# Clustered attention and its MoE layer: later chunks' query scale clipped, centroids' norm by Newton steps, a new order of work

## The chip, the cores and the metric

One core of one Trainium2 chip runs the whole program. The metric is the device time of one execution in microseconds (us). The kernel before took 847.42 us, the median of 3 runs (845.54 to 848.62). Five engines matter here: TensorE (PE, with its weight loads as PEld), VectorE (DVE), ScalarE (ACT), GpSimd (POOL), and SyncE (SP), whose one queue issues all DMAs of the loops.

## The reference

Four batches, eight heads, 768 tokens, head dimension 64, 16 centroids per head. Queries and keys are each given to the centroid with the largest cosine, and a query sees only keys of its own cluster. The outputs of all heads go through a two-layer network with the weights w_in (512 x 2048) and w_out (2048 x 512), which arrive as 64-bit floats.

```python
c_n = centroids / (np.linalg.norm(centroids, axis=-1, keepdims=True) + 1e-06)
q_assign = np.argmax(np.einsum('bhsd,hcd->bhsc', q_n, c_n), axis=-1)
k_assign = np.argmax(np.einsum('bhsd,hcd->bhsc', k_n, c_n), axis=-1)
mask = q_assign[:, :, :, None] == k_assign[:, :, None, :]
scores = np.where(mask, (1.0 / np.sqrt(D)) * np.matmul(q, k.transpose(0, 1, 3, 2)), -1e9)
attn = np.exp(scores - max);  attn = attn / (sum + 1e-09)
out = np.matmul(attn, v)
h = x @ w_in                      # x: the heads side by side, (3072, 512)
g = np.where(h >= 1, h, np.where(h <= -1, 0.0, (h + 1) ** 2 / 4))
return g @ w_out
```

## The kernel before

**Tiling.** Heads are taken in four pairs. The queries of a batch are cut into three chunks (c = 0, 1, 2) of 256 tokens, so there are 12 chunks, numbered u = 3b + c. For a chunk and a head pair there are four steps of scores (two heads, two blocks of 128 queries): four matmuls of 384 columns give the scores of 128 queries against 768 keys in PSUM, VectorE evicts them with a running minimum (tile sS), ScalarE takes the exponential, the result is split into a high and a low half-precision part (ScalarE, GpSimd), transposed by DMA, and multiplied with V. A finished chunk goes through the network in eight parts (ffn1, ffn2 of 256 hidden units each).

**Two stages.** Before its first use every weight has to be brought from 64-bit to 32-bit floats. `w_bits` does it with ScalarE (magnitudes) and VectorE (bit merges of 1024 words a partition), and only chunk 0 uses those 32-bit weights directly. Chunk 0's attention, the weights and the preparation of batch 0's keys and values share the opening; afterwards weights are split into two half-precision parts and all else runs from those.

**Scales.** Numbers are split into half-precision parts after a scaling by a power of two. `k_scale` (L807) keeps for each head pair the inverse scale `ik` and the scale `sc`; `q_scale` (L881) does so for the queries of a chunk (`iv`, `sc`). `q_split` (L896) forms the high and low parts of the scaled queries in the tile qn, and their transposes give `qT`. In `q_pairs` (L913) the one-hot of the cluster is appended, with the weight `ONE`, so that keys of other clusters fall out. The score's scale `es` is the product of the two inverse scales and the reference's 1/8, held away from zero at `ES_MIN`; where it is held, the factor phi = raw / es makes up for it, and it is multiplied into the queries everywhere: on GpSimd into the high part in its natural layout (4 instructions a chunk, the product taking the low part's place in the tile), on ScalarE into the transposed queries in place (4 a chunk). In chunks with c = 0 `q_pairs` is called once for each head pair, in the others once for all four.

**Centroids.** `centroids()` (L690) is the first work recorded: the sum of squares on VectorE, a square root on ScalarE, then the reciprocal and the scaling on VectorE, a split, and a DMA transpose into `cT`, which the first label matmuls read. The activation on the tile `tab` (L685 and L697) uses a function early so that its table is loaded before it is needed: Sqrt at the start, Exp after the norm.

**The order.** Nothing is issued as it is written. A recorder collects instructions as nodes of a graph with planned costs (`price`). `issue` (L391) runs a planner: `BASE` rounds of a forward pass (`forward`, the engine takes the ready node of the best priority) and a backward pass (`backward`, which gives every node a priority by its distance from the end). Then a list of seeds, `NUDGES`, moves the priorities of groups of events (an event is one call such as one head pair's `k_split`); `nudge` (L377) turns a seed into a group, a stride and a shift. A last forward pass fixes the order of every engine and of the DMA queue. Each instruction then waits for its data by semaphores. As all instructions go through the recorder, the profile puts them all on L405, and tiles tell them apart.

Of the kernel before, what the change touches and what calls it, by code (L numbers as in the profile page):

```python
# [11 lines left out]
F32 = mybir.dt.float32  # L12
# [34 lines left out]
BASE = 20  # L47
NUDGES = (
# [59 lines left out]


def mix(a):  # L110

    a &= 0xFFFFFFFF
    a ^= a >> 16
    a = a * 0x7FEB352D & 0xFFFFFFFF
    a ^= a >> 15
    a = a * 0x846CA68B & 0xFFFFFFFF
    return a ^ a >> 16


class Recorder:  # L120
# [256 lines left out]
    def nudge(self, seed, prio):  # L377

        a = mix(seed * 2654435761 + 1)
        b = mix(a + 1)  # L380
        c = mix(b + 1)
        names = sorted({x.ev for x in self.nodes})
        lo, every, size = b % len(names), (1, 2, 5)[(a >> 8) % 3], float(500 << ((a >> 16) % 5))
        at = {y: i for i, y in enumerate(names)}
        for x in self.nodes:
            i = at[x.ev]
            if lo <= i < lo + (1 << (a % 8)) and not (i - lo) % every:
                r = c if c >> 8 & 1 else mix(c + i * 7919)
                prio[x] += ((r & 0xFFFF) / 32768.0 - 1.0) * size

    def issue(self):  # L391
        for x in self.nodes:
            for y in x.preds:
# [172 lines left out]
def tile_clustered_attention_moe(  # L566
# [17 lines left out]
    P = 128  # L584
# [881 lines left out]
```

## Time and profile before

| | |
|---|---|
| device time, median of 3 runs | 847.42 us (845.54 to 848.62) |
| span of the profiled execution, first to last instruction | 844.9 us |
| the profiled execution's own time | not listed |
| TensorE matmuls busy | 807.8 us (96%), 7100 instructions |
| VectorE busy | 628.9 us (74%), 1390 instructions |
| ScalarE busy | 667.1 us (79%), 1175 instructions |
| GpSimd busy | 528.7 us (63%), 510 instructions |
| mean granted TensorE clock | 0.994 of full speed |
| bytes moved by DMA | 142.50 MB |

Busy time is the time in which an engine executes; the rest of the span it waits or has nothing to do. The profile's chain of waits, followed back from the last instruction, is 85% TensorE and 6% VectorE. The span in 40 slices shows TensorE at nine tenths or more from the fifth slice on and at two to seven tenths in the first four. Below, "idle before <-" is the time that an engine stood still in front of an instruction, and the instruction that ended it.

### The profile page before, as it was taken

How to read it: one execution, taken by the hardware profiler on the slowest of the kernel's cores; microseconds unless marked ns; L12 is line 12 of the kernel's file. 1: busy time of each engine (PE TensorE's matmuls, PEld its weight loads, DVE VectorE, ACT ScalarE, POOL GpSimd, SP SyncE). 2: the span in 40 equal slices, each digit the busy share in tenths (PEclk: the TensorE clock that was granted, in tenths of full speed). 3: DMA queues.
4: the chain of work that ended last, by engine and by line, in shares of the span. 5: the costliest groups of instructions: out<-in, count | busy, mean ns of one | idle time of the engine just before them, and what ended most of it. 6: DMA issues, size and time to landing. Idle time of an engine off the chain costs nothing.

```text
span 844.9 us, 18910 instructions
## 1 busy us (share of the span) xinstructions
PE 807.8 (96%) x7100; PEld 563.2 (67%) x7100; DVE 628.9 (74%) x1390; ACT 667.1 (79%) x1175; POOL 528.7 (63%) x510
## 2 busy tenths in 40 slices
PE   2677999999999999999999999999999999999998
PEld 2455677667676767666666767666676676667776
DVE  5999998788888758669888758678888767454331
ACT  7889999999988778788778778788778778776332
POOL 1012589888878668666667667666757668666312
PEclk9999999999999999999999999999999999999999
DMA  9977898979999799889999979999988767666100
GB/s 313 295 187 179 241 225 192 182 156 198 207 170 183 149 160 175 173 181 207 203 159 179 157 149 175 188 189 193 212 161 145 154 135 141 129 128 103 24 26 26
DMA packets 404907, 142.50 MB, mean 169 GB/s; under 512 B 372816, under 2 KB 396624, under 8 KB 404816
## 3 DMA queue, kind: packets, MB, share of 16 engines
q1 hardware_dynamic: 404816, 141.30, 82.0%
q8 instruction: 55, 0.90, 0.4%
q14 instruction: 36, 0.29, 0.1%
HBM read 40.40 MB, written 6.29 MB: 55 GB/s over the span
## 4 chain that ended last, share of the span: by engine, by line
PE 85%; DVE 6%; issue 2%; DMA 1%; ACT 1%; POOL 1%; SPq 0%; DVEq 0%; POOLq 0%; ACTq 0%
PE pair L405 42%; PE banka L405 12%; PE bankj L405 11%; PE banki L405 11%; PE bankh L405 9%; DVE sS L405 1%; DMA kv<-n 1%; DVE w L405 1%; DVE bankj L405 1%; DMA pT<-hl 1%; POOL hl L405 0%; DVE wk L405 0%; DVE x L405 0%; DVE mx L405 0%; DVE bankh L405 0%
## 5 line engine op out<-in xcount | busy, mean ns | idle before, releaser
L405 POOL TENSOR_TENSOR hl<-sS,hl 128x768 f16<-128x768 f32 x176 | 299.0, 1702 | 118.3 <-ACT hl L405 99.0
L405 PE MATMUL pair<-w,g 128*128 128x512 f16 (+2 forms) x1120 | 275.9, 387 | 0.0
L405 DVE CUSTOM_DVE_ANT_0 sS<-pair,zero,er 128x768 f32<-128x768 f32 x192 | 194.4, 1013 | 71.5 <-PE pair L405 57.7
L405 PEld LDWEIGHTS <-w 128*128 128x128 f16 x2112 | 205.6, 98 | 41.2 <-issue 2.0
L405 ACT ACTIVATE sS<-sS,sbi 128x768 f32<-128x768 f32 x192 | 179.1, 933 | 67.5 <-DVE sbi L405 64.9
L405 PEld LDWEIGHTS <-g 128*128 128x128 f16 x1104 | 105.5, 98 | 101.8 <-issue 1.4
L405 PE MATMUL pair<-kv,q 128*128 128x384 f16 x768 | 159.7, 332 | 5.6 <-ACT pT L405 3.3
L405 ACT CAST hl<-sS 128x768 f16<-128x768 f32 x176 | 144.7, 826 | 7.8 <-DMA pT<-hl 5.6
L405 POOL TENSOR_TENSOR g<-r,g 128x512 f16<-128x512 f32 x80 | 95.8, 1198 | 54.7 <-ACT g L405 54.5
L405 PEld LDWEIGHTS <-q 128*128 128x128 f16 x992 | 78.7, 98 | 62.8 <-issue 20.4
L405 PE MATMUL banka<-pT,kv 128*64 128x256 f16 (+1 forms) x1680 | 104.8, 279 | 0.0
L405 PEld LDWEIGHTS <-kv 128*64 128x64 f16 (+1 forms) x1824 | 92.6, 108 | 6.5 <-DMA kv<-n 2.6
L405 ACT ACTIVATE r<-r,f_ra,f_rs 128x512 f32<-128x512 f32 x80 | 64.8, 810 | 25.4 <-DVE r L405 24.8
L405 PE MATMUL bankj<-x,w 128*128 128x256 f16 (+1 forms) x424 | 58.3, 289 | 0.9 <-DVE r L405 0.9
L405 ACT CAST g<-r 128x512 f16<-128x512 f32 x80 | 48.9, 611 | 8.1 <-DVE r L405 7.1
L405 POOL TENSOR_TENSOR qn<-qn,phi 128x256 f16<-128x256 f16 x48 | 31.7, 676 | 36.3 <-DVE phi L405 27.2
L405 PE MATMUL bankh<-x,w 128*128 128x256 f16 (+1 forms) x376 | 46.7, 277 | 0.0
L405 PE MATMUL banki<-x,w 128*128 128x256 f16 (+1 forms) x288 | 40.0, 290 | 0.0
L405 ACT ACTIVATE q<-q,phi 128x512 f16<-128x512 f16 x48 | 33.6, 717 | 5.0 <-DVE phi L405 4.9
L405 PE MATMUL banki<-wk,w 128*128 128x256 f16 x312 | 37.2, 273 | 0.0
L405 ACT ACTIVATION_READ_ACCUMULATOR sS<-sS,sbi 128x1 f32 x192 | 36.1, 188 | 0.0
L405 POOL CAST rr<-rs 128x4 f16<-128x4 f32 x48 | 13.2, 276 | 36.1 <-DVE bankh L405 13.7
(269 smaller groups left out, 1114.8 us busy)
## 6 DMA issues: line engine op xcount, KB each, us to landing
w<-in_moe_w_out_dram SPq DMA_DIRECT2D x14, 512.0 KB, 5.8
q<-in_q_dram SPq DMA_DIRECT2D x12, 512.0 KB, 4.8
kv<-in_k_dram SPq DMA_DIRECT2D x16, 384.0 KB, 4.3
kv<-in_v_dram SPq DMA_DIRECT2D x16, 384.0 KB, 4.6
out_dram<-o SPq DMA_DIRECT2D x11, 512.0 KB, 3.6
w<-in_moe_w_in_dram SPq DMA_DIRECT2D x10, 512.0 KB, 7.3
word<-in_moe_w_in_dram SPq DMA_DIRECT2D x6, 512.0 KB, 6.0
o<-in_v_dram SPq DMA_DIRECT2D x8, 384.0 KB, 4.0
```

What stands on the lines that cost most here:

```text
L405: fn(*args, **kw)
```

## The change

Three things change. In chunks with c = 1 and 2 the queries' inverse scale `iv` is held from below, in `q_scale`, by a number worked out from the keys' scale `sk`, so that the score's scale is never under `ES_MIN`; the score's scale `es` is worked out there too, and phi, its GpSimd and its ScalarE multiplications are left out. The tile's low part is replaced by a copy of the high part on VectorE. Chunks with c = 0 stay as they were. `k_scale` keeps its scales in a tile for all four pairs (`sk`), in place of one small tile each.

The norm of the centroids is worked out on VectorE: a starting guess of 1/sqrt from the bits of the sum of squares, three Newton rounds of three instructions, and one product. The only early activation is an Exp.

The order comes from 37 rounds in place of 20, and from a list with one shift for every event, `SHIFTS`, added once to the priorities, in place of the seeds.

```diff
-BASE = 20
-NUDGES = (
-    4127111602, 1682835989, 681108749, 3292080817, 121738153, 2216588642, 619074244, 589741012, 2371205860,
...
+BASE = 37
+SHIFTS = (
+    -1711, 7131, 3865, 6139, 639, -10363, 2153, 2349, 9056, -1055, 6506, -1469, -561, 1610, 4832, -13174, -6658, 2275,
...
     def issue(self):
...
-        for seed in NUDGES:
-            self.nudge(seed, prio)
+        names = sorted({x.ev for x in self.nodes})
+        shift = dict(zip(names, SHIFTS, strict=True))
+        for x in self.nodes:
+            prio[x] += shift[x.ev]
         self.forward(prio)
...
-    rec.scalar.activation(out=tab, in_=ones[:, :1], func=AF.Sqrt)
+    rec.scalar.activation(out=tab, in_=ones[:, :1], func=AF.Exp, scale=0.0)
 
     def centroids():
...
-        nrm = const.tile([P, 1], F32, name="c_nrm")
-        rec.scalar.activation(out=nrm, in_=ss, func=AF.Sqrt)
-
-        rec.scalar.activation(out=tab, in_=nrm, func=AF.Exp, scale=0.0)
-        rn = const.tile([P, 1], F32, name="c_rn")
-        rec.vector.tensor_scalar(out=rn, in0=nrm, scalar1=1e-6, scalar2=None, op0=ALU.add)
+        rn, y, m = (const.tile([P, 1], F32, name=f"c_{x}") for x in ("rn", "y", "m"))
+
+
+        rec.vector.tensor_scalar(
+            out=y.bitcast(U32), in0=ss.bitcast(U32), scalar1=-0.5, scalar2=float(0x5F3759DF), op0=ALU.mult, op1=ALU.add
+        )
+        for _ in range(3):
+            rec.vector.scalar_tensor_tensor(out=m, in0=y, scalar=ss, in1=y, op0=ALU.mult, op1=ALU.mult)
+            rec.vector.tensor_scalar(out=m, in0=m, scalar1=-0.5, scalar2=1.5, op0=ALU.mult, op1=ALU.add)
+            rec.vector.tensor_tensor(out=y, in0=y, in1=m, op=ALU.mult)
+        rec.vector.tensor_scalar(out=rn, in0=ss, scalar1=y, scalar2=1e-6, op0=ALU.mult, op1=ALU.add)
         rec.vector.reciprocal(rn, rn)
...
-        sc = e["sc"] = new("sc", [1], F32, 2)
+        sc = e["sc"] = BX[b]["sk"][:, hp : hp + 1]
...
         rec.vector.tensor_scalar(out=iv, in0=ar, scalar1=TINY, scalar2=2.0**-11, op0=ALU.max, op1=ALU.mult)
+        if u % NCH:
+            f = BX[u // NCH]
+            es = e["es"] = new("es", [NP], F32, 2)
+            rec.vector.scalar_tensor_tensor(
+                out=iv, in0=f["sk"], scalar=ES_MIN / QK, in1=iv, op0=ALU.mult, op1=ALU.max
+            )
+            rec.vector.scalar_tensor_tensor(
+                out=es, in0=f["ik"], scalar=-QK, in1=iv, op0=ALU.mult, op1=ALU.mult
+            )
         rec.vector.reciprocal(sc, iv)
...
+        if c:
+            es = e["es"][:, pairs]
+            rec.vector.tensor_copy(nat[:, x, 0], nat[:, x, 1])
+        else:
+            raw, es = (ps[:, i * NP : i * NP + m] for i in range(2))
+            ph = new("phi", [NP], F32, 2)[:, :m]
...
```

## Rows read from the trace of the kernel before

**Rows 1.** Busy time by stretch: engines' busy us, granted clock, DMA share, GB/s.

```profile
0.00:15.00 15.00, 4.39 (x54) 3.67 (x55) 5.62 (x19) 9.44 (x17) 2.55 (x27) 1.00 0.88 283
15.00:95.00 80.00, 58.91 (x586) 40.32 (x582) 77.05 (x188) 70.31 (x111) 14.33 (x21) 0.94 0.90 244
95.00:800.00 705.00, 703.01 (x6153) 488.37 (x6152) 534.17 (x1168) 574.34 (x1030) 502.58 (x455) 1.00 0.86 167
800.00:845.00 45.00, 41.53 (x317) 30.82 (x315) 12.07 (x16) 12.99 (x20) 9.20 (x8) 1.00 0.06 24
```

**Rows 2.** Timeline, VectorE's long wait: start, us, instruction, [idle before <-releaser].

```profile
15.23 0.95 DVE L405 TENSOR_REDUCE v_am<-kv 128x1 bf16<-128x768 f32 x1 [2.78 <-DMA kv<-in_v_dram]
```

**Rows 3.** Timeline of TensorE, 78 to 102 us.

```profile
84.41 0.87 PE L405 MATMUL pair<-idf,sS 128*128 128x128 f32 x6 [1.43 <-ACT sS L405]
...
95.48 3.62 PE L405 MATMUL banki<-x,w 128*128 128x256 f32 x16
```

**Rows 4.** Timeline of VectorE, 78 to 102 us.

```profile
90.89 1.16 DVE L405 TENSOR_REDUCE aq<-q 128x4 bf16<-128x1024 f32 x1
91.98 0.94 DVE L405 TENSOR_REDUCE v_am<-x 128x1 bf16<-128x768 f32 x1
92.84 1.00 DVE L405 CUSTOM_DVE_ANT_0 sS<-pair,zero,er 128x768 f32<-128x768 f32 x1
```

**Rows 5.** VectorE's groups, 15 to 95 us: shape, count, busy us, mean ns.

```profile
L405 DVE SCALAR_TENSOR_TENSOR w<-w,o 128x1024 uint32<-128x1024 uint32 x5 | 6.1, 1222 | 0.0
...
L405 DVE SCALAR_TENSOR_TENSOR w<-word,wk 128x1024 uint32<-128x1024 uint32 x1 | 1.2, 1208 | 0.0
```

**Rows 6.** Timeline, all engines, the centroids' chain and the first labels.

```profile
6.25 0.08 DVE L405 DVE_READ_ACCUMULATOR2_ANT c_ss<- 128x1 f32 x1
...
7.63 0.19 ACT L405 ACTIVATE c_nrm<-c_ss 128x1 f32<-128x1 f32 x1
...
7.85 0.15 DVE L405 TENSOR_SCALAR c_rn<-c_nrm 128x1 f32<-128x1 f32 x1 [1.04 <-ACT c_nrm L405]
...
9.11 1.28 SPq L405 DMA_TRANSPOSE cT<-sS  x1
...
9.96 1.89 PE L405 MATMUL pair<-idf,qn 128*128 128x128 bf16 x16 [2.02 <-DVE qn L405]
...
10.48 0.92 ACT L405 ACTIVATE n<-kv,sc 128x768 f16<-128x768 f32 x1
11.42 1.28 ACT L405 ACT_TABLE_LOAD   x1
...
12.82 1.91 ACT L405 COPY q<-pair 128x1024 bf16<-128x1024 bf16 x2
...
13.87 0.60 PE L405 MATMUL bankj<-cT,q 128*128 128x16 f16 x16
...
14.79 0.60 PE L405 MATMUL bankj<-cT,q 128*128 128x16 f16 x16 [0.32 <-ACT q L405]
```

**Rows 7.** Timeline of VectorE, two dependent one-column instructions.

```profile
29.15 0.17 DVE L405 RECIPROCAL phi<-banki 128x1 f32<-128x1 f32 x1
29.35 0.16 DVE L405 TENSOR_TENSOR phi<-banki,phi 128x1 f32<-128x1 f32 x1
```

**Rows 8.** View of the tile cT: issue to landing.

```profile
DMA to landing us min/median/max: 4.5/4.5/4.5
```

**Rows 9.** View of the tile phi: ns min/median/max, first and last start.

```profile
L405 POOL TENSOR_TENSOR qn<-qn,phi x48: 603/612/1591, 20.3 to 701.0; 128x256 f16<-128x256 f16 x48
L405 ACT ACTIVATE q<-q,phi x48: 705/717/754, 20.8 to 708.9; 128x512 f16<-128x512 f16 x48
```

**Rows 10.** Timeline of VectorE, the one-hot of chunk 1's queries.

```profile
79.67 0.28 DVE L405 TENSOR_SCALAR qn<-zs 128x256 f16<-128x256 f32 x1
```

**Rows 11.** VectorE's groups by shape, whole span: the same conversion.

```profile
L405 DVE TENSOR_SCALAR qn<-zs 128x256 f16<-128x256 f32 x8 | 5.0, 626 | 0.1
```

**Rows 12.** Timeline of ScalarE, 78 to 90 us.

```profile
83.32 0.94 ACT L405 ACTIVATE sS<-sS,sbi 128x768 f32<-128x768 f32 x1 [0.24 <-DVE sbi L405]
```

More of the change, by code (lines that the diff above doesn't have):

```diff
@@ L46 @@
 LOOK, MARGIN = 0.4, 4000
-BASE = 20
-NUDGES = (
[56 rows of a table removed]
+BASE = 37
+SHIFTS = (
[54 rows of a table added]
 )
 TILED = 248
[L110 to L117, printed above, removed]
 class Recorder:
@@ L375, in backward @@
         return start
[L377 to L389, printed above, removed]
     def issue(self):
@@ L811, in k_scale @@
         if hp == 0:
-            BX.setdefault(b, {}).update(ik=new("ik", [NP], F32, 2), has=new("has", [NP, 2, C], F32))
+            BX.setdefault(b, {}).update(
+                ik=new("ik", [NP], F32, 2), sk=new("sk", [NP], F32, 2), has=new("has", [NP, 2, C], F32)
+            )
         am = new("am", [1], F32, 2)
@@ L893, in q_scale @@
         rec.vector.tensor_scalar(out=iv, in0=ar, scalar1=TINY, scalar2=2.0**-11, op0=ALU.max, op1=ALU.mult)
+        if u % NCH:
[6 more added lines that the diff above has]
+                out=es, in0=f["ik"], scalar=-QK, in1=iv, op0=ALU.mult, op1=ALU.mult
+            )
         rec.vector.reciprocal(sc, iv)
@@ L921, in q_pairs @@
         ps = misc(512)
-        raw, es, ri = (ps[:, i * NP : i * NP + m] for i in range(3))
         zq = view(ps[:, 64 : 64 + m * SC * C], [2 * m, CT, C], F32)
-        ph = new("phi", [NP], F32, 2)[:, :m]
-        rec.vector.scalar_tensor_tensor(
-            out=raw, in0=f["ik"][:, pairs], scalar=-QK, in1=e["iv"][:, pairs], op0=ALU.mult, op1=ALU.mult
-        )
-        rec.vector.tensor_scalar(out=es, in0=raw, scalar1=-ES_MIN, scalar2=None, op0=ALU.min)
-        rec.vector.reciprocal(ph, es)
-        rec.vector.tensor_tensor(out=ph, in0=raw, in1=ph, op=ALU.mult)
-        for i in range(m):
-            y = slice((hp + i) * SC, (hp + i + 1) * SC)
-            rec.gpsimd.tensor_tensor(
-                out=nat[:, y, 0], in0=nat[:, y, 1], in1=ph[:, i : i + 1].unsqueeze(2).to_broadcast([P, SC, D]), op=ALU.mult
-            )
-            qf = e["qT"][:, y].rearrange("p n q -> p (n q)")
-            rec.scalar.activation(out=qf, in_=qf, func=AF.Copy, scale=ph[:, i : i + 1])
+        if c:
[4 more added lines that the diff above has]
+            ph = new("phi", [NP], F32, 2)[:, :m]
+            rec.vector.scalar_tensor_tensor(
+                out=raw, in0=f["ik"][:, pairs], scalar=-QK, in1=e["iv"][:, pairs], op0=ALU.mult, op1=ALU.mult
+            )
+            rec.vector.tensor_scalar(out=es, in0=raw, scalar1=-ES_MIN, scalar2=None, op0=ALU.min)
+            rec.vector.reciprocal(ph, es)
+            rec.vector.tensor_tensor(out=ph, in0=raw, in1=ph, op=ALU.mult)
+            for i in range(m):
+                y = slice((hp + i) * SC, (hp + i + 1) * SC)
+                rec.gpsimd.tensor_tensor(
+                    out=nat[:, y, 0], in0=nat[:, y, 1], in1=ph[:, i : i + 1].unsqueeze(2).to_broadcast([P, SC, D]),
+                    op=ALU.mult,
+                )
+                qf = e["qT"][:, y].rearrange("p n q -> p (n q)")
+                rec.scalar.activation(out=qf, in_=qf, func=AF.Copy, scale=ph[:, i : i + 1])
         rec.vector.tensor_scalar(
```

108 rows, old and new, of tables (NUDGES, SHIFTS) are left out of this document.

## The prediction, made before the result was known

> **What bounds the kernel now.** I read the busy time by stretch first, because shares over the whole span mix stages with different limits. The sums of [rows 1] are to be read as TensorE idle time: 15.00 - 4.39 = 10.6 us before 15 us, 80.00 - 58.91 = 21.1 us from 15 to 95 us, 705.00 - 703.01 = 2.0 us from 95 to 800 us, and 45.00 - 41.53 = 3.5 us at the end; together 37.2 us, and 807.8 us of matmuls. From 95 us on TensorE is the bound: it is busy 99.7% of 705 us at the full clock of 2.4 GHz (granted 1.00), while ScalarE is busy 81%, VectorE 76% and GpSimd 71%. Work taken from those three there is worth nothing until it removes some of the 2.0 us. The last 3.5 us is one eviction and the store behind the last matmul.
>
> The stretch from 15 to 95 us is another kernel, and VectorE bounds it: 77.05 of 80 us busy, 2.95 us idle in all. Its one long wait, 2.78 us for the first V load, ends at 15.23 us and so lies almost wholly ahead of the stretch [rows 2]. ScalarE is close behind with 70.31 us; GpSimd has only 14.33. The granted clock is 0.94 there, so some 0.06 x 2 x 80 = 10 us ran at 1.2 GHz, which matters little while VectorE is late. What ends the stretch is told by the timeline: the first hidden-layer product of chunk 0 starts at 95.48 us with a 16-matmul group and from there TensorE never rests [rows 3]; it needs the four attention outputs of chunk 0, and in front of the last two score evictions (92.84 us) VectorE does a reduction of 1.16 us for chunk 2's queries and one of 0.94 us for the next batch's V [rows 4]. Neither is needed before 95 us. Twenty bit merges of weights, 1.22 us each, 24.5 us in all, are in the stretch too (the first and the last group of them in [rows 5]); that is where the order decides.
>
> **The change, part by part.** The matmuls stay as they are, 7100 of them, so TensorE's 807.8 us is a floor that nothing moves. The sum is made against the profiled execution: its span is 844.9 us, its own time is not listed, and the median of three runs is 847.4, so I add 2.5 us to any span.
>
> *Centroids.* Removed from ScalarE: the square root and the Exp on one element, 0.19 us each by the former's row, and the table load between two kinds of function, 1.28 us, together 1.66 us [rows 6]. It stands in a busy place: the K split ends at 11.40, the load runs from 11.42, and the copy of the transposed queries starts only at 12.82, though TensorE had transposed the queries by 9.96 + 1.89 = 11.85. Added to VectorE: one starting guess and three rounds of three, ten dependent instructions. Two dependent instructions on one column start 0.20 us apart [rows 7], so the norm is there 10 x 0.20 = 2.0 us after the sum of squares (6.33 us): 8.33 us against 7.85 now, 0.5 us later, and up to 0.8 us if the two instructions of the query scale stand between. The transposed centroids are issued at 9.11 and land 4.5 us after [rows 8], at 13.6 us, and the first label matmul starts at 13.87. So this wait, hidden behind ScalarE's copies by 0.2 us today, is what comes late next: landing at 14.1 to 14.4 us. All 32 label matmuls then run in one go, 1.2 us, and end at 15.3 to 15.6 us where they ended at 15.39. For the labels the two halves cancel: nothing. What is left is ScalarE's 1.66 us before 20 us, in a stage where it is the busier engine and prepares the magnitudes that VectorE merges later. The bounds are 1.66 us gained and 0.8 us lost; I take 0.7 us gained, under half, since VectorE, which ScalarE feeds, has only 2.95 us of idle time to give back before 95 us, and its wait before that is for a load.
>
> A rule of the Trainium skill gives this another price. The rows show a load of 1.28 us and the next activation running straight behind it [rows 6]. "ScalarE: Activation LUTs", What ACT_TABLE_LOAD costs, charges a switch of set with a drain of about 1.38 us as well, 2.66 us in total. By that rule ScalarE would be 1.38 us freer still and, at the same share, the gain 1.3 in place of 0.7 us, the time 843.8; here the trace disagrees, as no such gap stands around the load.
>
> *The factor phi.* It goes for 8 of 12 chunks: 32 of 48 GpSimd multiplications at a median 0.61 us and 32 of 48 ScalarE scalings at 0.72 us [rows 9], 20 and 23 us. With them go four small VectorE instructions a chunk (in the one call for all pairs); two new ones stand in the scale's step and one copy of 1024 half-precision numbers in place of the multiplication. The copy's price is not in the trace. From below: a conversion of 256 numbers into the same tile took 0.28 us with GpSimd idle [rows 10]; from above: the same conversion has a mean of 0.63 over the run [rows 11], where GpSimd competes, and 1.22 us is a two-input pass over 1024 words [rows 5]. I take 0.45 us, near the lower end, as in the opening GpSimd is idle. VectorE so pays -2 x 0.16 + 0.45 = +0.1 us a chunk, between -0.1 and +0.9. The copy has to wait until the queries' transpose has read the tile, as GpSimd's multiplication did; behind that nothing urgent stood on GpSimd, while on VectorE the next score eviction (1.00 us in [rows 4]) is queued, and TensorE waits for its bank. The upper bound is taken for that too.
> Seven of the eight chunks are prepared after 95 us, where TensorE is the bound: they give nothing. Chunk 1 alone is prepared in the opening. There ScalarE loses 4 x 0.72 = 2.9 us between 80 and 85 us, and TensorE does wait 1.43 us for a score exponential at 84.41 [rows 3]; but that exponential was itself waiting 0.24 us for VectorE [rows 12], so most of the wait is VectorE's. I take 0.4 us gained less 0.1 us for the copy: 0.3 us, with bounds of 0.9 us lost and 1.4 us (that wait) gained. Transposed queries no longer scaled in place can be read sooner, which takes part of the 2.0 us between 95 and 800 us: 0.3 us of it.
>
> *The order.* A priority list worked out anew moves everything, the loads and transposes on SP's one queue included, with less ScalarE and GpSimd work to place. No row prices it; the stretch bounds it. The two early reductions put behind 95 us are worth 1.16 + 0.94 = 2.1 us. Each weight merge put behind the last score eviction of chunk 0 is worth 1.22 us more, and each put ahead costs as much. I take 1.7 us gained: most of the two reductions, none of the merges. Its bounds are four merges more either way: 2.1 + 4.9 = 7.0 us gained, 4.9 us lost.
>
> Sum: 0.7 + 0.3 + 0.3 + 1.7 = 3.0 us; span 841.9 us, time 847.4 - 3.0 = **844.4 us**.
>
> **Rivals.** *The relief is hidden.* VectorE, not the relieved engines, bounds the opening, and TensorE the rest; the work on VectorE is the same to 2 us. Then only the 0.3 us from 95 us on remains: 847.1 us. For it speaks that 95 of 100 us of freed work lies where nobody waits; against it, that the centroid step frees ScalarE at its fullest.
> *The order brings chunk 0's products much earlier.* Both reductions and four merges go behind 95 us: 847.4 - 7.0 = 840.4 us. For it: 21.1 us of TensorE idle time lies in 80 us, and GpSimd, idle there, cannot be the limit. Against: the second-layer weights have to be merged in time for their own products, and the loads keep the DMA engines 0.90 busy.
> *The order puts VectorE work ahead of chunk 0's last scores.* The place is VectorE's queue before 95 us; each merge more costs 1.22 us there, and the other terms give 1.3 us back. From three on (3.7 - 1.3 = +2.4 us) it decides; with four 847.4 + 4.9 - 1.3 = 851.0 us. For it: an order fitted to planned costs can meet other ones on the chip, and VectorE has no slack to absorb it. Against: any list that does so leaves TensorE idle in its own plan.
>
> **How the numbers follow.** Forecast 0.42, with its own range from 842.5 to 846.5; hidden 0.21; much earlier 0.22; slower 0.15. The range should leave out half of the slower case and a third of the much earlier one: 839.0 to 849.5 us; it takes in the bounds of the copy and of the Newton chain. A measurement of this kernel tells 0.3% from no change, that is 2.5 us: faster is below 844.9, slower above 850.0. Faster: some 0.6 of the forecast's 0.42, all of 0.22 and a little of the hidden case, 0.51. Slower: 0.11, most of its case. Same: the rest, 0.38.
>
> **What would show it.** One table load in place of two, ten one-column instructions between the centroids' sum and their norm, and the transposed centroids landing after 14 us. TensorE's idle time from 95 us to the end within 0.5 us of today's 5.5; the whole difference in the opening. VectorE's busy time from 15 us to the first product of chunk 0 shorter by about 2 us, and that product at about 92.5 to 93 us, with the reductions for chunk 2 and the next batch behind it. GpSimd near 509 us and ScalarE near 642 us busy. I am wrong if the first product starts later than 95 us, if TensorE opens gaps of over 2 us after it, or if the busy time of TensorE itself changes.

## The result, and the profile after

The changed kernel took 853.31 us (median of 4 runs, 852.58 to 853.76), the kernel before on the same chip 847.61 us (4 runs, 845.54 to 848.62): ratio 1.0077, 95% interval 1.0062 to 1.0091. It is slower by some 6 us; the prediction of 844.4 us, its range up to 849.5 and its sign were wrong. The profiled execution of after has a span of 850.8 us and a time of 852.58 us, so 1.8 us lie around the span; the prediction had added 2.5.

Busy time of after by stretch, to be laid beside [rows 1] (stretch, its length, busy us of PE, PEld, DVE, ACT, POOL with counts, granted clock, DMA share, GB/s):

```profile
0.00:15.00 15.00, 3.96 (x32) 3.05 (x33) 8.01 (x31) 9.29 (x15) 2.48 (x27) 1.00 0.85 297
15.00:95.00 80.00, 59.08 (x589) 40.54 (x588) 73.98 (x181) 65.02 (x104) 8.94 (x17) 0.96 0.84 227
95.00:800.00 705.00, 699.93 (x6120) 484.46 (x6120) 532.68 (x1166) 558.21 (x1000) 484.37 (x426) 1.00 0.87 168
800.00:851.00 51.00, 47.38 (x362) 35.21 (x360) 13.64 (x19) 14.97 (x22) 10.34 (x9) 0.98 0.06 21
```

TensorE's idle time up to 95 us is 32.0 us, where it was 31.7. From 95 us on it is 5.07 + 3.42 = 8.5 us up to the end of the span, which lies 0.2 us before the end of the last row; it was 2.0 + 3.4 = 5.4. Its busy time rose by 2.5 us to 810.35 with the same 7100 matmuls; that alone is no sign of a loss, as in clip_no_copy_old_order below, which is no slower than the kernel before, they take 810.1 us. So 3.4 us more idle and 2.5 us more busy make the 5.9 us of the span. The opening was not idle for longer, but less was done in it: 14 matmuls that stood before 95 us come after it, six of scores and eight on a weight tile (TensorE's groups, 0 to 95 us, before and after: count | busy us, mean ns | idle just before, its releasers):

```profile
L405 PE MATMUL pair<-kv,q 128*128 128x384 f16 x86 | 20.9, 375 | 4.8 <-ACT pT L405 3.3 <-ACT kv L405 0.6 <-DVE sbi L405 0.6
L405 PE MATMUL bankj<-wk,ones 128*128 128x128 bf16 x16 | 1.2, 218 | 0.0
```

```profile
L381 PE MATMUL pair<-kv,q 128*128 128x384 f16 x80 | 19.8, 387 | 7.5 <-ACT pT L381 4.3 <-DMA kv<-x 2.0 <-ACT kv L381 1.1
L381 PE MATMUL bankj<-wk,ones 128*128 128x128 bf16 x8 | 0.6, 218 | 0.0
```

By these rows 1.1 + 0.6 = 1.7 us of work were pushed behind 95 us, so some 2 of the 5.9 us come out of the opening and some 4 arise after it. The first hidden-layer product does not show that share: it starts at 95.75 us against 95.48 [rows 3], and from there to the end of the span, the pushed-back work included, it is 850.8 - 95.75 = 755.1 us against 749.4. The relief came nearly as counted (ScalarE busy 647.5 us, GpSimd 506.1, where 642 and 509 were named), and nothing was faster for it.

What VectorE does in front of chunk 0's last scores, beside [rows 4], and the first product (timelines of VectorE and TensorE, after):

```profile
91.11 1.01 DVE L381 CUSTOM_DVE_ANT_0 sS<-pair,zero,er 128x768 f32<-128x768 f32 x1
92.05 1.21 DVE L381 TENSOR_REDUCE aq<-q 128x4 bf16<-128x1024 f32 x1
93.18 0.94 DVE L381 TENSOR_REDUCE v_am<-x 128x1 bf16<-128x768 f32 x1
94.04 1.01 DVE L381 CUSTOM_DVE_ANT_0 sS<-pair,zero,er 128x768 f32<-128x768 f32 x1
...
95.75 3.62 PE L381 MATMUL banki<-x,w 128*128 128x256 f32 x16
```

The two reductions that the prediction sent behind 95 us stand where they stood.

The centroids' chain, beside [rows 6] (timeline of VectorE, SyncE and TensorE, after):

```profile
5.48 0.15 DVE L381 TENSOR_SCALAR c_y<-c_ss 128x1 uint32<-128x1 uint32 x1
5.67 0.22 DVE L381 SCALAR_TENSOR_TENSOR c_m<-c_y,c_ss 128x1 f32<-128x1 f32 x1
6.93 0.14 DVE L381 TENSOR_SCALAR c_m<-c_m 128x1 f32<-128x1 f32 x1
...
9.90 0.21 DVE L381 TENSOR_SCALAR c_rn<-c_ss,c_y 128x1 f32<-128x1 f32 x1
...
12.01 1.28 SPq L381 DMA_TRANSPOSE cT<-sS  x1
15.96 1.00 PE L381 MATMUL bankj<-cT,q 128*128 128x16 f16 x32
```

The ten instructions begin 0.2 us apart where they follow each other, but the new order puts other work between them (1.26 us from the second to the third). The transpose goes out at 12.01 in place of 9.11 us, and the first label matmul waits until 15.96 in place of 13.87.

The clip's new instructions (VectorE's groups by shape, whole span: count | busy us, mean ns | idle just before, its releaser):

```profile
L381 DVE SCALAR_TENSOR_TENSOR iq<-sk,iq 128x4 f32<-128x4 f32 x8 | 5.6, 700 | 0.2
L381 DVE COPY qn<-qn 128x1024 f16<-128x1024 f16 x8 | 4.0, 499 | 7.2 <-DMA q<-qn 7.2
L381 DVE SCALAR_TENSOR_TENSOR es<-ik,iq 128x4 f32<-128x4 f32 x8 | 3.9, 487 | 0.0
```

The copy takes 0.50 us, near the 0.45 that was priced, but VectorE stands still for 7.2 us in front of the eight copies, for the queries' transpose. The two small instructions, priced at 0.16 us, take 0.49 and 0.70 on average.

TensorE's longest wait after the opening lies at 213 us (timeline of after, all engines; in brackets the wait in front of the instruction and what ended it):

```profile
205.74 2.12 POOL L381 TENSOR_TENSOR w<-word,w 128x1024 f16<-128x1024 f32 x1
205.83 2.12 DVE L381 TENSOR_TENSOR bankh<-zs,has 128x64 f32<-128x64 f32 x1
207.86 0.15 DVE L381 RECIPROCAL sk<-ik 128x1 f32<-128x1 f32 x1
208.05 0.94 ACT L381 ACTIVATE n<-kv,sk 128x768 f16<-128x768 f32 x1 [1.98 <-DVE sk L381]
...
210.21 1.42 SPq L381 DMA_TRANSPOSE kv<-n  x1
...
215.61 0.47 PE L381 MATMUL bankh<-cT,kv 128*128 128x32 f16 x12 [2.04 <-DMA kv<-n]
```

An addition on 64 columns, 0.22 us at its shortest in this kernel, lasts as long as GpSimd's pass beside it; the key scale queued behind it is 2 us late, and ScalarE, the transpose and TensorE pass that on. The Trainium skill, "SBUF — State Buffer", Who interferes with whom, says that a VectorE instruction with two SBUF inputs contends with a GpSimd instruction that reads SBUF, and that such contention is an exclusive lock. The two rows of 2.12 us agree: both inputs of the addition lie in SBUF, and it ends 0.1 us behind GpSimd's pass.

### The profile page after: what moved, and what is told of

It is laid out like the page before. It is cut to its first block, busy times and chain, and to the rows that moved or that the text cites. A ratio compares the mean times of both kernels' runs of the same rounds, so it can differ in the third digit from the quotient of the medians.

```text
span 850.8 us, 18823 instructions
## 1 busy us (share of the span) xinstructions
PE 810.4 (95%) x7100; PEld 563.3 (66%) x7100; DVE 628.3 (74%) x1392; ACT 647.5 (76%) x1140; POOL 506.1 (59%) x478
## 4 chain that ended last, share of the span: by engine, by line
PE 74%; DVE 9%; DMA 8%; ACT 4%; issue 3%; POOL 1%; SPq 0%; DVEq 0%; ACTq 0%; POOLq 0%
PE pair L381 37%; PE banka L381 11%; PE bankj L381 9%; PE bankh L381 9%; PE banki L381 8%; DMA pT<-hl 2%; DVE sS L381 2%; DMA kv<-x 1%; DMA kv<-n 1%; ACT sS L381 1%; DVE r L381 1%; DVE bankj L381 1%; DVE qn L381 1%; DVE bankh L381 1%; ACT hl L381 1%
## 5 line engine op out<-in xcount | busy, mean ns | idle before, releaser
L381 ACT CAST g<-r 128x512 f16<-128x512 f32 x80 | 48.7, 609 | 12.6 <-DVE r L381 10.3
L381 POOL CAST rr<-rs 128x4 f16<-128x4 f32 x48 | 10.5, 219 | 42.7 <-DVE w_sw L381 16.4
L381 DVE TENSOR_SCALAR r<-bankj,f_lo,f_hi 128x512 f32<-128x512 f32 x26 | 21.0, 808 | 14.2 <-PE bankj L381 10.8
L381 DVE TENSOR_SCALAR r<-bankh,f_lo,f_hi 128x512 f32<-128x512 f32 x27 | 21.8, 806 | 12.0 <-PE bankh L381 9.3
```

Source lines behind the costliest of these rows:

```text
L381: fn(*args, **kw)
```

## The experiments

In each of these kernels the order was taken from a plan in place of being searched: the start times that the planner of one of the two kernels had given its nodes. With a kernel's own plan this yields its own order on every engine. Instructions that the plan does not know go right behind what they need.

```diff
-        names = sorted({x.ev for x in self.nodes})
-        shift = dict(zip(names, SHIFTS, strict=True))
-        for x in self.nodes:
-            prio[x] += shift[x.ev]
-        self.forward(prio)
+        ...
+        heappush(heap, (when[x], x.i))    # when: planned start in the other kernel
```

One profile is one execution, and executions of a kernel differ by some 4 us (before: 844.6 to 849.0 over 28 of them), so differences below that are read from the ratios (4 to 12 executions of each kernel, beside 17 to 28 of the kernel before). The theory at first was that the order, not the two edits, costs the time; the rival was the edits.

**Edits and order apart.** Both edits with the order before; the work before with the new order; each edit alone with the order before.

> All edits of the change to the work itself (clipped scale, copy, Newton steps), with the order of the kernel before kept: every instruction that both have stands in its old place on its engine, the new ones are put in behind what they need. Theory A, the new order loses: the edits by themselves are worth next to nothing, so 845 to 849 us (ratio to before 0.997 to 1.002), no more than 3 us of TensorE idle time between 95 us and 840 us. Theory B, the edits lose (the Newton chain puts the transposed centroids late, the copies on VectorE delay score evictions): 851 to 855 us in this order too.

Measured: 850.91 us, ratio 1.0045 (1.0029 to 1.0061), between the theories: the edits do cost time, 3.8 us, but not all of the loss.

> The work of the kernel before (phi everywhere, square root on ScalarE) in the order of the changed kernel; the removed instructions are put in behind what they need. Theory A, the order loses: 851 to 856 us, with some ten TensorE stalls over 0.25 us between 100 and 835 us as in the changed kernel. Theory B, the edits lose: 846 to 849 us, three such stalls as before.

Measured: 872.95 us, ratio 1.0300 (1.0281 to 1.0318), far above both bands. TensorE waits 19.5 us in all between 110 and 835 us, where it waits 4.8 in the changed kernel. That the new order relies on the relief is argued from this, not shown: the work put back stands right behind what it needs, and other places for it were not tried.

> Only the centroids' norm by Newton steps and one table load less, in the old order. Theory A: the transposed centroids land some 0.5 to 1 us later, ScalarE is 1.7 us freer, 846 to 849 us. Theory B: 849 to 853 us, the first product of chunk 0 over 1 us later than 95.5 us.

Measured: 847.19 us, ratio 1.0005 (0.9993 to 1.0017), with the transpose out at 9.75 us and the first label matmul at 13.68. The Newton steps are worth nothing that can be told from zero, between 0.6 us gained and 1.4 us lost.

> Only the clipped scale, the copy in place of the multiplications by phi, in the old order. Theory A: 845.5 to 848.5 us, since all that goes is on engines that nobody waits for. Theory B: 849 to 852 us, VectorE's copies stand in front of score evictions and TensorE stalls behind them.

Measured: 850.45 us, ratio 1.0039 (1.0026 to 1.0051). The clip, meant as a relief, costs 3.3 us with the order untouched. Its eight copies and their idle time (VectorE's groups), one of them, and what TensorE does after it (timeline of VectorE and TensorE):

```profile
L681 DVE COPY qn<-qn 128x1024 f16<-128x1024 f16 x8 | 4.6, 579 | 10.3 <-DMA q<-qn 10.3
```

```profile
648.54 0.91 DVE L681 COPY qn<-qn 128x1024 f16<-128x1024 f16 x1 [1.94 <-DMA q<-qn]
649.37 0.41 DVE L681 TENSOR_TENSOR rb<-banka,rb 128x256 f32<-128x256 f32 x1
649.70 1.00 DVE L681 CUSTOM_DVE_ANT_0 sS<-pair,zero,er 128x768 f32<-128x768 f32 x1
650.76 0.81 PE L681 MATMUL pair<-kv,q 128*128 128x384 f16 x4 [1.06 <-DVE sbi L681]
```

VectorE stands 1.94 us for the transpose, copies for 0.91 us, and a score eviction queued behind both comes late; TensorE waits 1.06 us for its bank.

**The copies moved late, the norm moved early.** In the first three, each copy goes right in front of the one-hot that follows it in its chunk; in the fourth, the ten Newton instructions are kept together, in the new order.

```diff
+for e in chunks: plan[e, "copy qn"] = plan[e, "one-hot qn"] - 1
```

> The run clip_in_old_order again (only the clipped scale, the old order), the same instructions, with one thing moved: each of the eight copies on VectorE stands directly in front of the one-hot conversion, behind the labels, in place of right behind the splits. By then the transpose that still reads the tile has landed. Theory C, the copy's wait for that transpose blocks VectorE's queue (10.3 us of idle time in eight waits): VectorE's wait falls under 1 us, the TensorE stalls at 460 and 650 us go, 846.0 to 848.0 us in place of 850.5. Theory D, the copy's own work and its effect on GpSimd cost the time: the work is the same, 849.5 to 851 us.

Measured: 848.97 us, ratio 1.0023 (1.0012 to 1.0034). This lies between the theories. VectorE no longer waits for the transposes, and some 1.4 of the 3.3 us are back, though the two intervals overlap. The copies' own time did not fall (4.6 us); one of them lasts until a pass of GpSimd is over (timeline of GpSimd and VectorE):

```profile
143.09 1.65 POOL L681 TENSOR_TENSOR hl<-sS,hl 128x768 f16<-128x768 f32 x1
143.49 1.53 DVE L681 COPY qn<-qn 128x1024 f16<-128x1024 f16 x1
```

> All edits (clip and Newton steps), the old order, the copies directly in front of the one-hot conversions. Theory C: 845.5 to 847.5 us, the first product of chunk 0 at 95.0 to 95.5 us as with the Newton steps alone; if a version beats both kernels, it is this one. Theory D: 850 to 851.5 us as edits_in_old_order.

Measured: 849.08 us, ratio 1.0030 (1.0018 to 1.0041), between the theories too; the gain that Theory C foresaw did not come.

> The changed kernel in its own order, with the eight copies alone moved directly in front of the one-hot conversions. Theory C: the 7.2 us of VectorE's waits go and with them some 2 to 3 us: 850.0 to 851.5 us; what is then left against 847.1 is the new order. If the waits in this order stand where nobody is late: 852.5 to 853.5 us, and the order has all of the loss.

Measured: 858.55 us, ratio 1.0140 (1.0125 to 1.0155), above both bands. The same move that helps in the old order costs 5 us in the new one. The first product starts at 94.47 us there, 1.3 us earlier than in after, and 855.3 - 94.47 = 760.8 us follow it.

> The changed kernel in its own order, with the Newton chain alone moved: its steps follow each other in VectorE's queue in place of being spread behind the query splits, so that the transposed centroids are issued at about 9.8 us in place of 12.0. Theory E, the late centroids (first label at 15.96 in place of 13.87 us) put the opening back: first label before 14.2 us, first product of chunk 0 some 0.5 to 1 us earlier than 95.75, 852.0 to 852.8 us. Rival, VectorE is the bound from 13 us on and fills the wait with weight merges: 853.0 to 853.8 us, first product within 0.3 us of 95.75.

Measured: 854.65 us, ratio 1.0084 (1.0068 to 1.0099), above both bands. The theory that the late centroids cost the time fell. The first product starts at 94.04 us, 1.7 us earlier than in after, and the span is 853.4: 759.4 us follow. In this execution the later stage gave back what the opening gained.

**The copy taken off VectorE.** One GpSimd copy in place of VectorE's, where the plan had the first multiplication (in the fourth kernel, the new order, where it had the copy); and the copy left out, so that the later chunks' label term reads the queries' low part.

```diff
-            rec.vector.tensor_copy(nat[:, x, 0], nat[:, x, 1])
+            rec.gpsimd.tensor_copy(nat[:, x, 0], nat[:, x, 1])
```

> The clip alone, in the order before, with the copy of the queries' high part done by GpSimd as one instruction at the place of its first multiplication, in place of VectorE. Theory A (the clip costs time because VectorE's in-order queue holds score evictions behind the copy: 1.5 us for its wait, and the rest for the 0.4 to 0.9 us that it takes): 847.0 to 848.0, ratio 1.000 to 1.001, no VectorE wait on the queries' transpose. Rival B (the freed GpSimd and ScalarE start their other work earlier, and GpSimd's two-input passes then lie beside VectorE's passes that TensorE waits for): 848.5 to 850, ratio 1.002 to 1.004, with stretched VectorE passes in front of the stalls.

Measured: 847.97 us, ratio 1.0006 (0.9995 to 1.0017).

> The clip alone, in the order before, with the copy left out for the eight later chunks (the queries that the label term reads are then the low part). Nothing stands in place of the multiplications, so this is the whole relief without its price. Theory A: 846.0 to 847.5, ratio 0.999 to 1.0005, a little faster than the version with the copy on GpSimd. Rival B: as slow as with the late copy, 848.5 to 850, ratio 1.002 to 1.004, since the relief itself shifts the passes of GpSimd against those of VectorE.

Measured: 847.41 us, ratio 1.0003 (0.9992 to 1.0014). Theory A held: with the copy off VectorE, or gone, the clip costs nothing measurable, and the relief gains nothing measurable either. The shifted passes of GpSimd (rival B) are not the cause.

> Both edits in the order before, with the copy on GpSimd: the candidate to keep. Theory A: the Newton steps are worth nothing to 0.4 us, so 846.5 to 848.0, ratio 0.9995 to 1.001. Rival B: 848.5 to 850.5, ratio 1.002 to 1.004.

Measured: 846.00 us (12 runs), before 847.02 (28 runs), ratio 0.9991 (0.9982 to 1.0001). This is the best version of the study; it is not shown to be faster than the kernel before. Its copies (GpSimd's groups) and its first product (timeline of TensorE):

```profile
L681 POOL COPY qn<-qn 128x1024 f16<-128x1024 f16 x8 | 9.3, 1158 | 0.0
```

```profile
94.03 3.19 PE L681 MATMUL banki<-x,w 128*128 128x256 f32 x14
```

A copy costs GpSimd 1.16 us, less than the four multiplications of 0.61 us that it replaces [rows 9].

> The changed kernel in its own order, with the copy on GpSimd at the place in time where that order had VectorE's copy. Theory A: VectorE's 7.2 us of waits for the queries' transpose go, a part of which TensorE felt: 850.5 to 852.5, ratio 1.004 to 1.0065. Rival B (this order has no slack for GpSimd either: its passes behind the copy come late, or collide elsewhere): 853 to 857, ratio 1.007 to 1.012.

Measured: 854.62 us, ratio 1.0088 (1.0067 to 1.0110). Theory A missed: in the new order the same cure brings nothing. With the same instructions, the new order costs 854.6 - 846.0 = 8.6 us.

**The two halves of the order.** Both edits, copy on GpSimd, and the two plans joined at 95 us (12 nodes lie on different sides of it in the two plans).

```diff
+when[x] = first[x] if first[x] < 95000 else second[x]
```

> Both edits with the copy on GpSimd; what is planned before 95 us in the order before, everything after it in the changed order. Theory A (the loss of the changed order is mostly the run of small TensorE stalls after 95 us, which has no tie to the opening): 850.5 to 853, ratio 1.004 to 1.007. Rival B (the loss comes from the opening, and the later stalls follow from its lateness): 846 to 848, ratio 0.999 to 1.001.

Measured: 853.90 us, ratio 1.0082 (1.0066 to 1.0097). Theory A: the opening is as early as in the best version (first product at 94.43 us), and the later stage alone costs 853.9 - 846.0 = 7.9 us (7.7 by the ratios). The time is above Theory A's band: it foresaw a smaller loss.

> The other half: what is planned before 95 us in the changed order, everything after it in the order before, copy on GpSimd. Theory A: the opening alone costs what the traces show at 100 us, 3.0 us more than the same edits in the order before (846.0): 848 to 850, ratio 1.002 to 1.004. Rival B: all of the loss, 853 to 855.5, ratio 1.007 to 1.010.

Measured: 856.85 us (852.03 to 857.78), ratio 1.0098 (1.0079 to 1.0116), above both bands. The profile is of its fastest execution, at 852.03 us; where the others lose up to 5.8 us more was not seen. In that profile 4.5 us are one wait at the seam, for a VectorE pass that is one of the 12 nodes (timeline of VectorE and TensorE):

```profile
95.89 1.78 DVE L681 TENSOR_SCALAR wk<-wk 128x1024 uint32<-128x1024 uint32 x1
97.73 0.77 PE L681 MATMUL bankj<-wk,ones 128*128 128x128 bf16 x8 [4.46 <-DVE wk L681]
```

What TensorE waits for between 110 and 835 us, in this kernel (us in total, times, longest):

```profile
PE bankj L681 <- DVE r L681: 1.0, 1, 1.0
PE pair L681 <- DVE sbi L681: 0.8, 1, 0.8
```

and in the one with the new order there:

```profile
PE pair L676 <- DVE sbi L676: 2.1, 5, 0.7
PE bankh L676 <- DMA kv<-n: 2.0, 1, 2.0
PE banka L676 <- DMA pT<-hl: 1.0, 1, 1.0
PE banki L676 <- DVE r L676: 1.0, 2, 0.6
PE bankh L676 <- DVE er L676: 0.4, 1, 0.4
PE bankh L676 <- DVE zs L676: 0.3, 1, 0.3
PE banka L676 <- POOL rr L676: 0.2, 1, 0.2
```

With the old order in the later stage, two kinds of wait are left, 1.8 us, as in the best version (2.0 us in the kernel before), although the opening ran 6.8 us late. With the new one there are twelve, 7.0 us, behind an opening that was early. So the waits belong to the order of the later stage; of the 851.1 - 843.5 = 7.6 us between the spans of the early-opening kernel and the best version they are 7.0 - 1.8 = 5.2. What the new opening costs without a seam is not shown: even the fastest execution here is 852.0 - 846.0 = 6.0 us behind the best version, and 4.5 of them are the seam.

**One wait of the new order, and the prediction's own step.** In the changed kernel the key scale's reciprocal goes ahead of the addition; and, in the best version, the two reductions go behind the last two score evictions.

```diff
+plan[key pair, "reciprocal sk"] = 203620
```

> The changed kernel with one reciprocal on one column (the key scale of one pair, at 204 to 208 us) put ahead of the addition that took 2.12 us beside GpSimd's pass. Theory A (the 2.0 us wait of TensorE at 213 us comes from that addition's place): the wait goes, 851.3 to 852.5, ratio 1.005 to 1.006. Rival B (the next late thing takes its place): 852.8 to 854, ratio 1.007 to 1.008.

Measured: 852.84 us, ratio 1.0064 (1.0047 to 1.0082), by the ratio between the theories. The wait at 213 us fell from 2.04 to 1.28 us: the reciprocal came first, but the key's second half still stood behind the same 2.11 us addition.

```diff
+plan["aq of chunk 2"], plan["v_am of batch 1"] = 93800, 93820
```

> Both edits with the copy on GpSimd in the order before, and the two VectorE reductions of 1.16 and 0.94 us (next queries, next V) moved behind the last two score evictions of chunk 0, as the prediction took the changed order to do. The prediction's price: 2.1 us less than 846.0, so 843.5 to 844.5, ratio 0.996 to 0.997. Rival B (the first products are held by ScalarE or the transposes too, or the late reductions stall something else): 845.5 to 848, ratio 0.9985 to 1.001.

Measured: 847.73 us, ratio 1.0004 (0.9995 to 1.0012). Rival B: no gain. Timeline of VectorE and TensorE:

```profile
91.17 1.48 PE L681 MATMUL pair<-kv,q 128*128 128x384 f16 x8
92.03 1.02 DVE L681 CUSTOM_DVE_ANT_0 sS<-pair,zero,er 128x768 f32<-128x768 f32 x1 [1.06 <-PE pair L681]
...
93.91 1.22 DVE L681 TENSOR_REDUCE aq<-q 128x4 bf16<-128x1024 f32 x1
...
94.69 1.46 PE L681 MATMUL banki<-x,w 128*128 128x256 f32 x6
95.04 0.95 DVE L681 TENSOR_REDUCE v_am<-x 128x1 bf16<-128x768 f32 x1
95.90 0.42 DVE L681 SCALAR_TENSOR_TENSOR x<-banka,rb 128x256 f32<-128x256 f32 x1
...
96.37 2.43 PE L681 MATMUL banki<-x,w 128*128 128x256 f32 x10 [0.22 <-DVE x L681]
...
104.52 0.17 PE L681 MATMUL banki<-aq,ones 128*128 128x4 bf16 x1 [1.16 <-DVE g L681]
```

In front of the score VectorE now stands idle 1.06 us, because TensorE has not yet made the product: half of the 2.1 us was never VectorE's to give. The rest went into an attention output that came behind the reductions, so that the first product broke in two, and into a later wait of 1.16 us for another pass of VectorE.

## Why the prediction was wrong

Two steps failed, the term of the order and the term of the copy, and how the loss divides between them depends on where the copy stands. With the copy on VectorE, as in the change, the edits alone lose 3.8 us (1.3 gained was said) and the new order 2.7 us more by the ratios; with the copy on GpSimd the edits lose nothing and the order has the whole loss. All three signs of being wrong that the prediction named came: a first product later than 95 us (which the kernel before had as well), a wait of over 2 us after it, and a changed busy time of TensorE. This last is neither a floor nor fixed: the same 7100 matmuls take 806.4 to 813.9 us in the profiles of this study.

**The order.** +1.7 us gained was said, and with the same instructions, copy on GpSimd, the new order loses 8.6 us. Two things in the term were wrong. The stage: the bounds (7.0 gained, 4.9 lost) were taken from the opening alone, and the new order of the later stage by itself loses 7.9 us, in a stage that the prediction had set aside with "TensorE is the bound" and 2.0 us of idle time. That small idle time was a product of the old order, not a property of the stage; it could shrink by 2.0 us at most and grow by far more. And the price: the two reductions were not moved by the change, and where they are moved by hand, 2.1 us become nothing. That VectorE bounds the opening was read from its busy share, but at the end of the opening TensorE and VectorE take turns.

**The factor phi** failed in its copy. Its size was right (0.45 us said, 0.50 measured). The wait in front of it was named and put into the upper bound of 0.9 us a chunk, but then only for the one chunk in the opening, while "seven of the eight chunks ... give nothing". They give nothing, but they can take: in the order before, each of the eight copies waits 1.3 us on average (10.3 / 8) at the head of VectorE's queue, with score evictions behind it. By the ratios the clip costs 3.3 us with the copy on VectorE and 0.5 with it on GpSimd, so 2.8 us are the copy's. Moving it late takes back about half, which is the wait; taking it off VectorE brings the rest. Whether that rest is the copy's own time in the queue or its meeting with GpSimd's passes is not shown. In the changed kernel itself the copy is not a separate loss: on GpSimd there, it comes out at 854.6 in place of 853.3 us. The 3.3 us and the 8.6 us do not add up; the new order was made with the copy on VectorE in it, and with the copy there it costs 2.7 us more than the old one (1.0077 against 1.0045).

**The centroids** came out nearly as said for the labels: with the Newton steps alone the first label matmul starts at 13.68 us, where it was 13.87. That is in part luck of one execution: the transpose went out at 9.75 in place of 9.11 us but landed 3.8 us after, where the prediction took 4.5 [rows 8]. The term of +0.7 us is not borne out; it lies just outside the interval (1.0005, 0.9993 to 1.0017, or 0.6 us gained to 1.4 lost). That the transposed centroids land 1.5 us later still than the predicted 14.4 us is the order's doing, and the earlier norm brought no time back.

**The relief** of ScalarE and GpSimd was counted nearly right and rightly held to be worth next to nothing after 95 us; its two terms of 0.3 us cannot be told from zero (1.0003, 0.9992 to 1.0014, with the copy gone). The rival "hidden" (847.1 us) is what the edits do with the copy off VectorE. The slower rival (851.0 us) had the right sign and, for the most part, the wrong place: VectorE's queue before 95 us, where most of the loss lay after it.

Still open is which decisions of the new order's later stage matter. Its waits are many and small; one was made shorter, and 0.5 us by the medians or 1.1 by the ratios came back, with intervals that overlap. The late copy cost 5 us more in this order, and the other two moves, the early norm and the copy on GpSimd, changed nothing beyond the intervals. What the new opening costs by itself is open too. With the norm early, the profiled first product came 1.7 us sooner and the whole was no shorter; what holds the later stage there besides TensorE was not found.

## What to carry to other kernels

Where the bound engine is 99.7% busy, idle time of the others has no price, but the place of an instruction in their queues has: one that waits for a DMA holds everything behind it, so put it on the engine whose queue nobody needs soon, and ask that for every repetition, not only where you look for gains. A stage with hardly any idle time can gain by a new order no more than that idle time and can lose far more, so its range must reach to the slow side by what the order hides, not by the idle time that is left. Price an edit with the old order first, and the new order with the same instructions; here that separates a neutral norm, a costly copy and a costly order.

## What was not expected of the hardware

A VectorE addition of 64 columns took 0.22 us at its shortest and 2.12 us beside a GpSimd pass of 2.12 us; two VectorE instructions on four columns took 0.49 and 0.70 us on average, where the one-column instructions of [rows 7] took 0.16 and 0.17. A half-precision copy of 1024 columns on VectorE took 0.40 to 0.47 us in the opening, with GpSimd idle, and up to 1.53 us beside a GpSimd pass; on GpSimd it took 1.16 us.
